# Writing the first batch's front in a fixed order on four engines, with constant tables split on the host

## The chip, the cores and the metric

One core of one Trainium2 chip. The metric is the device time of one execution in microseconds; the time before is the median of three runs. The profile is one further execution, whose engines are TensorE (PE), VectorE (DVE), ScalarE (ACT) and GpSimd (POOL); SyncE (SP) issues the DMAs of before.

## The reference

Eight batches, eight heads, 576 positions, head dimension 64, 32 packing queries; all in fp32. A first attention packs the keys and values with the 32 queries, a second attention reads the packed values with 576 queries. The result, [8, 576, 512], goes through a block that mixes by a two-dimensional Fourier transform and then through a feed-forward network (FFN).

```python
p_packed = sm_attn(p, k, v)
x = sm_attn(q, p_packed, p_packed)        # heads joined: [8, 576, 512]
u = x + real(fft(fft(x, axis=1), axis=2))
un = (u - mean(u)) / sqrt(var(u) + 1e-6)
out = u + relu(un @ w_ch1) @ w_ch2        # 512 -> 2048 -> 512
```

## The kernel before

Products that need more than one reduced-precision pass are made from a hi and a lo part of each operand, in three matmuls (`three`): hi x hi, hi x lo, lo x hi. `split` makes the parts: ACT casts the hi part, DVE or POOL subtracts it for the lo part. On DVE this reads `yl<-py,yh`, on POOL `wr_l<-w1f,wr_h`.

`front(b)` computes one batch from its attention to `u`. The heads are handled in two groups, 0 and 1, of four heads each. The pieces have letters, and the string `ORDER` says in which order they are written: K, V, Q load keys, values and queries; s scores and exponentials of the first attention (`s1`, `e1`), t their transposes, p the packed values (`po`, `pp2`, and the block-diagonal `bd`, `bdh`, `bdl`), d the transposed packed values, q scores of the second attention, e subtraction of the maximum and exponentials (`less_one`), m subtraction of the mean (`less_mean`), a normalisation `s*z` and transpose (`weights`), f sums and differences `eo` and `f` of mirrored positions (`folded`), r small remaining sums (`folded_rest`), h hi and lo parts `fh`, `fl`, `xl`, `ol`, g the cosine and sine spectrum of the values over the columns (`turned`, then `gh`, `gl`), B and T the constant tables `basis` and `tbh`, `tbl`, `tbr`. After the pieces, products `py` of `fh` with `gh` of both groups give `yh`, `yl` and `yr`; products `pz` of those with the tables give the spectrum `spec`, products `px` the values themselves; and `pe`, `qe` are joined to `u` in the buffer `ubuf`. A batch gives four blocks of 128 tokens (two pairs) and half a block of rest (the R rows). `statistics` gives mean and variance of each block: ACT squares (`junk`) and a power on POOL.

The FFN runs over nine tiles of four blocks. For a tile the normalised blocks `un` are transposed on PE (`untp`) and split into `uh` and `ul`. `up(j)` makes 12 matmuls into `ph` and their relu `hh`, `hl`; `down(j-1)` makes 12 matmuls into four accumulators `acc`; j runs from 0 to 15. Behind each, `step(i)` writes the next part of the front of the following batch, so batch 1's front lies in tile 0. Weights arrive as 64-bit numbers, two 32-bit words each (512 KB for 128x512), in `wst` or a spare place (`w1f`, `w2f`, `ubuf`), and are made into fp32 by one ACT and two DVE instructions (`load_weights`, L171); each place is loaded again when DVE has read it. `wsplits` splits each weight chunk into `wr_h` (ACT) and `wr_l` (POOL).

From tile 1 on, the order of each engine's instructions is the order in which the program is written (`manual_schedule`). Batch 0's front and tile 0 with batch 1's front are given to a scheduler, which orders them by its own estimates. The DMAs of SP go out in the order of one queue.

The tables `EN`, `EF`, `ES`, `EO` choose DVE (0) or POOL (1) by batch (first, second, others) and group.

Of the kernel before, what the change touches and what calls it, by code (L numbers as in the profile page):

```python
# [9 lines left out]
F32 = mybir.dt.float32  # L10
# [6 lines left out]
P = 128  # L17
# [21 lines left out]
ORDER = ("K0 I0 K1 B0 V0 V1 Q0 Q1 W0 W1 W2 W3 s0 t0 p0 d0 s1 t1 p1 q0 e0 d1 g0 q1 e1 m0 m1 a0 f0 r0 h0 a1 "  # L39
         "f1 r1 h1 g1 T0",  # L40
# [37 lines left out]
def tile_kernel(ctx, tc, kpT, qT, v, w1, w2, tabC, tabS, tabR, tabB, tabT, sel, ident_d, out):  # L78
# [44 lines left out]

    def load_base():
        nc.sync.dma_start(sels, sel)
        st = load(tabB, [P, 2, N2], "st_base", "wst")
        h = work.tile([P, 2, N2], F32R, tag="tmp", name="base_h", bufs=3)
        nc.scalar.copy(h, st)
        nc.vector.scalar_tensor_tensor(basis, h.bitcast(F32), selC, st, ALU.mult, ALU.add)
        nc.sync.dma_start(turn, tabT)  # L130

    def load_tables():
        for t, d in enumerate((tabC, tabS)):
            st = load(d, [P, 1, KT], "st_tab", (t, 2))
            split(tbh[t], tbl[t], st[:, 0, :])
        st = work.tile([P, 2, 320], F32, tag="wst", name="st_tabr", bufs=2)
        nc.sync.dma_start(st[:101], tabR)
        for t in range(2):

            h = work.tile([P, DM], F32R, tag="tmp", name="tabr_h", bufs=3)  # L140
            nc.scalar.copy(h[:101, :320], st[:101, t, :])
            nc.vector.scalar_tensor_tensor(
                tbr[t][:101], h[:101, :320].bitcast(F32), selA[:101], st[:101, t, :], ALU.mult, ALU.add)
# [25 lines left out]
    def load_weights(j):  # L169

        for n, dst in enumerate((w1f, w2f)):  # L171
            if (j, n) not in fetched:
                fetch(j, n)
            st = fetched.pop((j, n))
            low, high = st[:, :, 0], st[:, :, 1]
            c = dst[:, j, :].bitcast(I32)


            nc.scalar.activation(c.bitcast(F32), high.bitcast(F32), AF.Prelu, scale=REBIAS, alpha=-2.0 ** 32)  # L179
            nc.vector.tensor_scalar(c, c, 3, None, ALU.logical_shift_left)  # L180
            nc.vector.scalar_tensor_tensor(c, low, 29, c, ALU.logical_shift_right, ALU.bitwise_or)  # L181
# [59 lines left out]
    def front(b):  # L241
# [75 lines left out]
        def packed(g):  # L317
# [15 lines left out]
            bd = work.tile([P, 4, D], F32, tag="tmp", name="bd", bufs=3)  # L333
            nc.gpsimd.tensor_tensor(bd, pp2[:, 0:1, :].to_broadcast([P, 4, D]),
                                    bmask.unsqueeze(2).to_broadcast([P, 4, D]), ALU.mult)

            def diagonals():
                bdh[g] = work.tile([P, 4 * D], F32R, tag="bdh", name="bdh")
                bdl[g] = work.tile([P, 4 * D], F32R, tag="bdl", name="bdl")
                split(bdh[g], bdl[g], bd.rearrange("p a d -> p (a d)"), nc.gpsimd)  # L340

            after(1, diagonals)

        def packed_parts(g):
# [10 lines left out]
            nc.vector.tensor_tensor(lo, tp[:, :P], hi.bitcast(F32), ALU.subtract)  # L355
# [44 lines left out]
        def values_spectrum(g):  # L400
# [21 lines left out]

        def weights(g):

            engs[g].tensor_tensor(s2s[g], s2s[g], broadcast(zs[g]), ALU.mult)
# [48 lines left out]
        def folded_parts(g):  # L474
# [17 lines left out]
                 "W": lambda i: fetch(i // 2, i % 2), "D": load_weights}  # L492
# [7 lines left out]
        yh, yl, yr = [], [], []  # L500
        for t, base in enumerate((0, FO)):
# [24 lines left out]
        def spectrum(t, par):  # L526

            pz = bank("pz")
            k0, off = (0, 0) if par is not None else (P, rows.start)
            pars = (0, 1) if par is None else (par,)  # L530
            for i, q in enumerate(pars):
                w = slice(KW * q + k0 - off, KW * q + k0 - off + P)
                three(pz[:, :N2], tbh[t][:, w], tbl[t][:, w], yh[t][:, q, :], yl[t][:, q, :], i == 0, False)
            k0 = KW * par if par is not None else k0
            nc.tensor.matmul(pz[:, :N2], tbr[t][:NRC[t], k0 - off:k0 - off + P], yr[t][:NRC[t]], start=False, stop=True)
            sb = work.tile([P, N2], F32, tag=f"spec{t}", name=f"spec{t}", bufs=1)
            nc.scalar.copy(sb, pz[:, :N2])
            return sb

        def value(ah, al, w):  # L540
            px = bank("px")
            for g in range(2):
                three(px[:, g * 256:(g + 1) * 256], ah[g][:, w], al[g][:, w], bdh[g], bdl[g], True, True)
            return px

        def window(sb, rows):
            w = sb[rows, 0:256]
            return bass.AP(tensor=w.tensor, offset=w.offset, ap=[list(w.ap[0]), [1, 2], [1, 256]])

        allp = slice(0, P)  # L550

        def halves(x):
            return x.rearrange("p (a c) -> p a c", a=2)

        for c in range(2):
            A, Bs = spectrum(0, c), spectrum(1, c)
            yield
            px = value(xh, xl, slice(1 - c, 256, 2))
            pe = work.tile([P, DM], F32, tag="tmp", name="pe", bufs=3)
            nc.vector.tensor_tensor(halves(pe), halves(px), window(A, allp), ALU.add)  # L560
            px = value(oh, ol, slice(1 - c, 256, 2))
# [8 lines left out]
            statistics((b, "O", c))  # L570
            yield (None, "rest")[c]
# [138 lines left out]

    gen0 = front(0)
# [140 lines left out]
```

## Time and profile before

| | us |
|---|---|
| runs | 1027.53, 1029.04, 1028.04 |
| median | 1028.04 |
| span of the profiled execution | 1025.3 |
| PE busy in it | 978.5 (95%) |
| DVE busy | 608.8 (59%) |
| ACT busy | 425.0 (41%) |
| POOL busy | 463.1 (45%) |
| first matmul of the first up-projection `ph` | 62.70 |
| first output of tile 0 issued | 187.99 |

The profile gives, for the profiled execution, a span from the first to the last instruction; the time of a run is measured around that execution, and the median lies 2.7 us above this span. In rows of the timeline the first number is the start from the span's beginning, the second the length, then engine, line, operation, tile written and tiles read, and shapes. In the chain of waits each row is a piece of the work that ended last, with what it waited for ahead of it.

### The profile page before, as it was taken

The page shows a single profiled execution, that of the slowest core. Times are in us where ns is not written, and L with a number is a line of the kernel's source. Part 1 is how long each engine was busy: PE and PEld are TensorE (multiplying, and loading weights), DVE is VectorE, ACT ScalarE, POOL GpSimd, SP SyncE. Part 2 cuts the span into 40 slices and gives each one's busy share as a digit, 9 for nine tenths or more (in the row PEclk, how much of TensorE's full clock was granted, in tenths as well). Part 3 has the DMA queues.
Part 4 walks back from the last instruction along what each step waited for, and adds up shares of the span by engine and source line. Part 5 has one row for each costly group of instructions (what it writes and reads, how often), then busy time and mean ns, then how long its engine had stood idle before and what let it go on. Part 6 is the DMA issues. An engine that isn't in the chain of part 4 may idle for free.

```text
span 1025.3 us, 14876 instructions
## 1 busy us (share of the span) xinstructions
PE 978.5 (95%) x5692; PEld 795.6 (78%) x5692; DVE 608.8 (59%) x1264; ACT 425.0 (41%) x883; POOL 463.1 (45%) x419
## 2 busy tenths in 40 slices
PE   6489889999999999999999999999999999999998
PEld 2367668878877888788887887788778888887886
DVE  3897994559465856677556846594658562114112
ACT  2556454444443434444444435444435343333322
POOL 1535635364335534454345533643355344444443
PEclk9699899999999999999999999999999999999999
DMA  8328440220023000310041002200210000001001
GB/s 329 109 64 280 157 123 1 93 96 1 1 78 111 1 1 34 108 48 1 1 140 49 1 1 93 96 0 1 82 58 0 1 26 17 0 1 43 1 1 42
DMA packets 17742, 58.64 MB, mean 57 GB/s; under 512 B 2081, under 2 KB 2465, under 8 KB 17670
## 3 DMA queue, kind: packets, MB, share of 16 engines
q1 hardware_dynamic: 17670, 57.68, 16.4%
q8 instruction: 45, 0.74, 0.3%
q14 instruction: 27, 0.22, 0.1%
HBM read 48.24 MB, written 9.44 MB: 56 GB/s over the span
## 4 chain that ended last, share of the span: by engine, by line
PE 76%; DVE 11%; ACT 5%; DMA 3%; issue 2%; POOL 2%; ACTq 0%; SPq 0%; DVEq 0%; POOLq 0%
PE ph L647 35%; PE acc L664 30%; DVE ubuf L567 2%; DMA wst<-w 2%; DVE turned L419 1%; ACT hh L653 1%; PE po L326 1%; PE s L269 1%; ACT junk L217 1%; DVE turned L415 1%; POOL wr_l L100 1%; PE e1tp L303 1%; DVE hl L654 1%; ACT wr_h L99 1%; DVE w2f L181 1%
## 5 line engine op out<-in xcount | busy, mean ns | idle before, releaser
L100 POOL TENSOR_TENSOR wr_l<-w1f,wr_h 128x512 fp32r<-128x512 f32 x144 | 190.8, 1325 | 398.9 <-ACT wr_h L99 395.1
L654 DVE SCALAR_TENSOR_TENSOR hl<-ph,hh 128x512 fp32r<-128x512 f32 x144 | 98.8, 686 | 305.3 <-ACT hh L653 305.0
L647 PE MATMUL ph<-uh,wr_h 128*128 128x512 f32 (+1 forms) x580 | 231.5, 399 | 11.8 <-DVE hl L654 9.6
L100 POOL TENSOR_TENSOR wr_l<-w2f,wr_h 128x512 fp32r<-128x512 f32 x144 | 192.4, 1336 | 91.9 <-ACT wr_h L99 91.9
L664 PE MATMUL acc<-wr_l,hh 128*128 128x512 f32 x576 | 227.0, 394 | 3.0 <-POOL wr_l L100 3.0
L647 PE MATMUL ph<-uh,wr_l 128*128 128x512 f32 (+1 forms) x580 | 229.3, 395 | 0.4 <-POOL wr_l L100 0.4
L647 PE MATMUL ph<-ul,wr_h 128*128 128x512 f32 (+1 forms) x580 | 229.3, 395 | 0.2 <-DVE ul L100 0.2
L664 PE MATMUL acc<-wr_h,hh 128*128 128x512 f32 x576 | 227.8, 396 | 0.0
L664 PE MATMUL acc<-wr_h,hl 128*128 128x512 f32 x576 | 226.2, 393 | 0.0
L653 ACT ACTIVATE hh<-ph 128x512 fp32r<-128x512 f32 x144 | 85.8, 596 | 285.6 <-PE ph L647 285.4
L647 PEld LDWEIGHTS ph<-uh,wr_h 128*128 128x128 f32 x580 | 109.9, 190 | 44.9 <-DVE hl L654 9.8
L647 PEld LDWEIGHTS ph<-uh,wr_l 128*128 128x128 f32 x580 | 110.0, 190 | 24.7 <-POOL wr_l L100 0.8
L664 PEld LDWEIGHTS acc<-wr_l,hh 128*128 128x128 f32 x576 | 108.2, 188 | 26.8 <-POOL wr_l L100 5.4
L647 PEld LDWEIGHTS ph<-ul,wr_h 128*128 128x128 f32 x580 | 110.0, 190 | 23.9 <-issue 1.7
L664 PEld LDWEIGHTS acc<-wr_h,hh 128*128 128x128 f32 x576 | 108.2, 188 | 23.5 <-ACT w2f L179 0.8
L664 PEld LDWEIGHTS acc<-wr_h,hl 128*128 128x128 f32 x576 | 108.2, 188 | 23.1
L99 ACT CAST wr_h<-w2f 128x512 fp32r<-128x512 f32 x144 | 89.4, 621 | 9.4 <-PE ph L647 7.8
L99 ACT CAST wr_h<-w1f 128x512 fp32r<-128x512 f32 x144 | 88.4, 614 | 8.0 <-PE ph L647 3.1
L217 ACT ACTIVATE junk<-ubuf,stat 128x512 f32<-128x512 f32 x36 | 25.8, 718 | 77.3 <-DVE stat L213 77.3
L608 PE MATMUL untp<-ident,un 128*128 128x128 f32 x144 | 37.2, 273 | 1.9 <-DVE stat L220 1.7
L100 POOL TENSOR_TENSOR gl<-turned,gh 128x516 fp32r<-128x516 f32 x16 | 25.2, 1573 | 22.1 <-ACT gh L99 22.1
L567 DVE SCALAR_TENSOR_TENSOR ubuf<-qe,pe 128x512 f32<-128x512 f32 x32 | 34.6, 1115 | 0.5
(199 smaller groups left out, 1292.8 us busy)
## 6 DMA issues: line engine op xcount, KB each, us to landing
kp<-kpT SPq DMA_DIRECT2D x16, 608.0 KB, 4.9
out<-ubuf SPq DMA_DIRECT2D x36, 256.0 KB, 2.1
vt<-v SPq DMA_DIRECT2D x14, 640.0 KB, 4.7
wst<-w SPq DMA_DIRECT2D x17, 512.0 KB, 4.0
qt<-qT SPq DMA_DIRECT2D x14, 576.0 KB, 4.8
ubuf<-w SPq DMA_DIRECT2D x9, 512.0 KB, 4.6
w1f<-w SPq DMA_DIRECT2D x3, 512.0 KB, 11.1
w2f<-w SPq DMA_DIRECT2D x3, 512.0 KB, 11.2
```

Of the source, the lines that this page charges most:

```text
L99: nc.scalar.copy(hi, src)
L100: (lo_eng or nc.vector).tensor_tensor(lo, src, hi.bitcast(F32), ALU.subtract)
L181: nc.vector.scalar_tensor_tensor(c, low, 29, c, ALU.logical_shift_right, ALU.bitwise_or)
L217: nc.scalar.activation(junk, u, AF.Square, bias=st[:, 1:2], scale=-1.0, accum_out=st[:, 2:3])
L269: nc.tensor.matmul(res[g][c][at, :w.stop - w.start], lhs(g, h), rhs(g, h, w), start=True, stop=True, tile_position=(r, h * NPK))
L303: nc.tensor.transpose(tp[g][:, c * P:(c + 1) * P], e1s[g][:, c * P:(c + 1) * P], ident)
L567: nc.vector.scalar_tensor_tensor(u_of[key], qe, sign, pe, ALU.mult, ALU.add, accum_out=stat_of[key][:, 0:1])
L608: nc.tensor.transpose(tp[:, c * P:(c + 1) * P], un[:, c * P:(c + 1) * P], ident)
L647: nc.tensor.matmul(ph[:, t], l[:, c * P:(c + 1) * P], r[:, c, t], start=(k == 0), stop=(k == 11))
L653: nc.scalar.activation(hh[:, :T], ph[:, :T], AF.Relu)
L654: nc.vector.scalar_tensor_tensor(hl[:, :T], ph[:, :T], 0.0, hh[:, :T].bitcast(F32), ALU.max, ALU.subtract)
L664: nc.tensor.matmul(acc[i], l[:, w], r, start=(j == 0 and k == 0), stop=(j == NJ - 1 and k == 2))
```

## The change

Batch 0's front and the turning of its four blocks are written under `manual_schedule`, in an order given by the first string of `ORDER`. Tile 0 itself stays with the scheduler.

- New pieces: x exponentials of the first attention apart from its maxima, b `bd` and its parts, l the lo part of the packed values, j the join of the turned spectrum with its parts, w and v the two halves of rebuilding a weight (ACT; DVE), c the parts of `basis`, z the next weight split, P the products `py` of one group. All 18 products of group 0 are written ahead of those of group 1, in six banks.
- The table `EW` is new, and `EF` changed: `s*z` and `eo` of batch 0's group 1 go from POOL to DVE.
- `tbh`, `tbl` and `tbr` are no longer split on the core. Their hi and lo parts come from the host, and six DMAs on POOL's queue load them (4 x 224 KB, 2 x 160 KB); the three loads on SP go.
- `un` of the first four blocks is made by ACT (Identity with the negative mean as bias) instead of DVE.
- The squares and deviations of batch 0's blocks are put off to steps 6 and later of tile 0, and the R rows of batch 0 to its steps 0 and 2.
- The order of loads on SP is another for batch 0.

```diff
-EF = (((0, 0, 0, 0), (1, 1, 0, 0)), ((1, 1, 1, 1), (0, 0, 0, 0)), ((0, 0, 0, 0), (0, 0, 0, 0)))
+EW = ((0, 0), (1, 0), (0, 0))
+EF = (((0, 0, 0, 0), (0, 0, 0, 0)), ((1, 1, 1, 1), (0, 0, 0, 0)), ((0, 0, 0, 0), (0, 0, 0, 0)))
...
-ORDER = ("K0 I0 K1 B0 V0 V1 Q0 Q1 W0 W1 W2 W3 s0 t0 p0 d0 s1 t1 p1 q0 e0 d1 g0 q1 e1 m0 m1 a0 f0 r0 h0 a1 "
-         "f1 r1 h1 g1 T0",
+ORDER = ("K0 K1 V0 I0 Q0 V1 W0 Q1 B0 W1 W2 W3 s0 x0 s1 t0 x1 p0 t1 d0 w0 v0 q0 e0 p1 l0 d1 c0 m0 q1 b0 T0 a0 e1 "
+         "g0 f0 r0 w1 l1 m1 w2 w3 g1 z0 a1 j0 h0 P0 f1 r1 b1 j1 h1 P1",
...
     def load_tables():
-        for t, d in enumerate((tabC, tabS)):
-            st = load(d, [P, 1, KT], "st_tab", (t, 2))
-            split(tbh[t], tbl[t], st[:, 0, :])
-        st = work.tile([P, 2, 320], F32, tag="wst", name="st_tabr", bufs=2)
-        nc.sync.dma_start(st[:101], tabR)
         for t in range(2):
-            h = work.tile([P, DM], F32R, tag="tmp", name="tabr_h", bufs=3)
-            nc.scalar.copy(h[:101, :320], st[:101, t, :])
-            nc.vector.scalar_tensor_tensor(
-                tbr[t][:101], h[:101, :320].bitcast(F32), selA[:101], st[:101, t, :], ALU.mult, ALU.add)
+            nc.gpsimd.dma_start(tbh[t], tabH[t])
+            nc.gpsimd.dma_start(tbl[t], tabL[t])
+            nc.gpsimd.dma_start(tbr[t], tabR[t])
...
-        after(1, squares)
-        after(2, deviation)
+        if steps[0] is None:
+            n = 6 + 2 * len(due) // 2
+            due.extend([(n, squares), (n + 1, deviation)])
+        else:
+            after(1, squares)
+            after(2, deviation)
...
+        def in_place(kind, g, what):
+            if b == 0:
+                late[kind, g] = what
+            else:
+                what()
...
-            engs[g].tensor_tensor(s2s[g], s2s[g], broadcast(zs[g]), ALU.mult)
+            engw[g].tensor_tensor(s2s[g], s2s[g], broadcast(zs[g]), ALU.mult)
...
+        def first_products(g):
+            outs = [(0, 0), (0, 2), (1, 0), (1, 2), (0, 1), (1, 1)]
+            if g == 0:
+                ypx.update({o: bank("py") for o in outs})
...
+            for t, c in outs:
+                py = ypx[t, c]
+                nr, base = NRC[t] if c == 2 else P, (0, FO)[t]
+                w = slice(base + c * P, base + c * P + nr)
+                three(py[:nr, :N2], fh[g][:, w], fl[g][:, w], gh[g][:, t, :], gl[g][:, t, :], g == 0, g == 1)
...
+        if b == 0:
+            ypx["q", 0] = odd_values(0)
+            spec = {(t, c): spectrum(t, c, "wr" if c else None) for c in range(2) for t in range(2)}
+            ypx["p", 1] = value(xh, xl, slice(0, 256, 2))
+            ypx["q", 1] = odd_values(1)
+            for c in range(2):
+                blocks(c, even(c, spec[0, c], ypx["p", c]), spec[1, c], ypx["q", c])
+                yield ("means", "rest")[c]
...
-    for at in gen0:
-        if at == "rest":
-            break
-    cur = Turned(tiles[0][1])
-    for i in range(4):
-        cur.less(i)
-        for move in cur.moves(i):
-            move()
-        cur.parts(i)
-    for _ in gen0:
-        pass
+    def turn_blocks(*ks):
+        for i in ks:
+            key = cur.keys[i]
+            cur.un[i] = work.tile([P, DM], F32, tag="ln", name="un")
+            nc.scalar.activation(cur.un[i], u_of[key], AF.Identity, bias=stat_of[key][:, 1:2])
+        for i in ks:
+            for move in cur.moves(i):
+                move()
+
+    with tc.manual_schedule(engines=MANUAL):
+        for at in gen0:
+            if at == "means":
+                turn_blocks(0, 1)
+            elif at == "rest":
+                break
+        cur.parts(0)
+        cur.parts(1)
+        bits(1, 0)
+        turn_blocks(2, 3)
+        cur.parts(2)
+        cur.parts(3)
+        next(splits)
+        bits(0, 1)
+        bits(1, 1)
...
-    rest = iter(())
+    rest = gen0
...
-            if t > 0 and i in (0, 2):
+            if i in (0, 2):
                 next(rest, None)
```

Three places of the order follow. The first is POOL in batch 0, between the lo part of the first block-diagonal (`bdl`) and the subtraction of the maximum from the second attention's scores of group 1 (L381, which is L410 now). Before:

```order
L100 TENSOR_TENSOR bdl<-bd,bdh 128x256
L334 TENSOR_TENSOR bd<-pp_238,bmask 128x256
L100 TENSOR_TENSOR bdl<-bd,bdh 128x256
L100 TENSOR_TENSOR gl<-turned,gh 128x516
L381 TENSOR_TENSOR s_298<-s_298,m_301 128x576
L397 TENSOR_TENSOR s_298<-s_298,d_314 128x576
```

Now:

```order
L101 TENSOR_TENSOR bdl<-bd,bdh 128x256
L140 DMA tbh_87<-tabH 128x448
L141 DMA tbl_89<-tabL 128x448
L142 DMA tbr_93<-tabR 128x320
L140 DMA tbh_88<-tabH 128x448
L141 DMA tbl_90<-tabL 128x448
L142 DMA tbr_94<-tabR 128x320
L410 TENSOR_TENSOR s_281<-s_281,m_299 128x576
L489 TENSOR_TENSOR f<-eo 128x3x15 x4
```

Group 1's block-diagonal and group 0's `gl` have left this place, and the six table loads stand in it; group 0's small sums stand between the two subtractions of group 1.

The second place is DVE from group 1's lo part `fl` to the first pair of `u` (`s_`, `spec_` and the like carry numbers of the program's buffers). Before:

```order
L485 TENSOR_TENSOR fl<-f,fh 128x776
L100 TENSOR_TENSOR tbl_89<-w1f,tbh_87 128x448
L100 TENSOR_TENSOR tbl_90<-w2f,tbh_88 128x448
L142 SCALAR_TENSOR_TENSOR tbr_93<-tabr_h,sels,st_tabr 101x320
L142 SCALAR_TENSOR_TENSOR tbr_94<-tabr_h,sels,st_tabr 101x320
L100 TENSOR_TENSOR yl<-py,yh 128x258 x2
L518 SCALAR_TENSOR_TENSOR yr<-yr_h,sels,pyr 101x258
L100 TENSOR_TENSOR yl<-py,yh 128x258 x2
L518 SCALAR_TENSOR_TENSOR yr<-yr_h,sels,pyr 99x258
L560 TENSOR_TENSOR pe<-px,spec_487 128x512
L181 SCALAR_TENSOR_TENSOR w1f<-w1f 128x512
L563 TENSOR_TENSOR qe<-px,spec_494 128x256
```

Now:

```order
L519 TENSOR_TENSOR fl<-f,fh 128x776
L101 TENSOR_TENSOR yl<-py,yh 128x258
L585 SCALAR_TENSOR_TENSOR yr<-yr_h,sels,py 101x258
L101 TENSOR_TENSOR yl<-py,yh 128x258
L585 SCALAR_TENSOR_TENSOR yr<-yr_h,sels,py 99x258
L101 TENSOR_TENSOR yl<-py,yh 128x258 x2
L625 TENSOR_TENSOR pe<-px,spec_505 128x512
L630 TENSOR_TENSOR qe<-px,spec_512 128x256
```

The table parts and the weight's bits are gone from this stretch.

The third place is PE around the first up-projection, where `s_706` (now `s_682`) are batch 1's first scores. Before:

```order
L269 MATMUL s1t<-kp 32x64 x4
L269 MATMUL s_706<-kp 32x512 x4
L608 MATMUL untp<-ident,un 128x128 x8
L269 MATMUL s1t<-kp 32x64 x4
L608 MATMUL untp<-ident,un 128x128 x4
L647 MATMUL ph<-uh,wr_h 128x256
L647 MATMUL ph<-ul,wr_h 128x256
L647 MATMUL ph<-uh,wr_l 128x256
```

Now, with the 21 rows of that up-projection from L731 on left out between the two pieces:

```order
L290 MATMUL s1t<-kp 32x64
L731 MATMUL ph<-uh,wr_h 128x256
L290 MATMUL s1t<-kp 32x64 x3
L692 MATMUL untp<-ident,un 128x128 x8
L731 MATMUL ph<-ul,wr_h 128x256
```

```order
L731 MATMUL ph<-uh,wr_l 128x256
L748 MATMUL acc_613<-wr_h,hh 128x512
L748 MATMUL acc_613<-wr_l,hh 128x512
L290 MATMUL s_682<-kp 32x512 x4
L290 MATMUL s1t<-kp 32x64 x4
```

Batch 1's first scores moved from ahead of the up-projection to behind the first two matmuls of the first accumulator, and the R rows' products `px`, which stood ahead of these rows, follow behind the second up-projection.

More of the change, by code (lines that the diff above doesn't have):

```diff
@@ L167, in fetch, with chunk, top, bits @@
         fetched[j, n] = st
-    def load_weights(j):
[L171 to L181, printed above, removed]
+    def chunk(j, n):
+        return (w1f, w2f)[n][:, j, :].bitcast(I32)
+    def top(j, n):
+        if (j, n) not in fetched:
+            fetch(j, n)
+        high, c = fetched[j, n][:, :, 1], chunk(j, n)
+        return nc.scalar.activation(c.bitcast(F32), high.bitcast(F32), AF.Prelu, scale=REBIAS, alpha=-2.0 ** 32)
+    def bits(j, n):
+        low, c = fetched.pop((j, n))[:, :, 0], chunk(j, n)
+        nc.vector.tensor_scalar(c, c, 3, None, ALU.logical_shift_left)
+        nc.vector.scalar_tensor_tensor(c, low, 29, c, ALU.logical_shift_right, ALU.bitwise_or)
+    def load_weights(j):
+        for n in range(2):
+            tc.keep_in_program_order(top(j, n))
+            bits(j, n)
     u_of, stat_of, place_of, free = {}, {}, {}, list(range(NU))
@@ L332, in packed, with spread, diagonals @@
             pp2s[g] = pp2
[L333 to L342, printed above, removed]
+            def spread():
+                bd = work.tile([P, 4, D], F32, tag="tmp", name="bd", bufs=3)
+                nc.gpsimd.tensor_tensor(bd, pp2[:, 0:1, :].to_broadcast([P, 4, D]),
+                                        bmask.unsqueeze(2).to_broadcast([P, 4, D]), ALU.mult)
+                def diagonals():
+                    bdh[g] = work.tile([P, 4 * D], F32R, tag="bdh", name="bdh")
+                    bdl[g] = work.tile([P, 4 * D], F32R, tag="bdl", name="bdl")
+                    split(bdh[g], bdl[g], bd.rearrange("p a d -> p (a d)"), nc.gpsimd)
+                after(1, diagonals)
+            in_place("b", g, spread)
         def packed_parts(g):
@@ new lines, in spectrum @@
+        def spectrum(t, par, tag=None):
+            pz = bank("pz")
+            k0, off = (0, 0) if par is not None else (P, rows.start)
+            pars = (0, 1) if par is None else (par,)
+            for i, q in enumerate(pars):
+                w = slice(KW * q + k0 - off, KW * q + k0 - off + P)
+                three(pz[:, :N2], tbh[t][:, w], tbl[t][:, w], yh[t][:, q, :], yl[t][:, q, :], i == 0, False)
+            k0 = KW * par if par is not None else k0
+            nc.tensor.matmul(pz[:, :N2], tbr[t][:NRC[t], k0 - off:k0 - off + P], yr[t][:NRC[t]], start=False, stop=True)
+            sb = work.tile([P, N2], F32, tag=tag or f"spec{t}", name=f"spec{t}", bufs=6 if tag else 1)
+            copied = nc.scalar.copy(sb, pz[:, :N2])
+            if b == 0 and par is None:
+                tc.keep_in_program_order(copied)
+            return sb
@@ L497, in front @@
                 parts[x[0]](int(x[1:] or 0))
-        yh, yl, yr = [], [], []
-        for t, base in enumerate((0, FO)):
+        for t, base in enumerate((0, FO) if b else ()):
             nr = NRC[t]
@@ L523, in front, with even, blocks @@
             yield
[L526 to L558, printed above, removed]
+        def even(c, A, px):
             pe = work.tile([P, DM], F32, tag="tmp", name="pe", bufs=3)
             nc.vector.tensor_tensor(halves(pe), halves(px), window(A, allp), ALU.add)
-            px = value(oh, ol, slice(1 - c, 256, 2))
+            return pe
+        def blocks(c, pe, Bs, px):
             qe = work.tile([P, DM], F32, tag="tmp", name="qe", bufs=3)
```

104 lines of the change are left out of this document (78 added, 26 removed).

## The prediction

> **What bounds the kernel now.** I read first the busy time by stages (columns: stretch and its length; busy microseconds and instructions of PE, weight loads, DVE, ACT, POOL; granted clock of PE; DMA share; GB/s).
>
> ```profile
> 0.00:63.00 63.00, 36.67 (x301) 24.75 (x301) 43.73 (x107) 28.84 (x67) 20.96 (x49) 0.84 0.52 183
> 63.00:104.00 41.00, 38.92 (x265) 28.73 (x265) 33.14 (x68) 22.29 (x45) 21.21 (x18) 0.96 0.65 220
> 104.00:144.00 40.00, 30.73 (x135) 23.45 (x134) 39.34 (x80) 18.06 (x33) 21.47 (x19) 0.87 0.35 113
> ...
> 188.00:300.00 112.00, 111.17 (x675) 91.48 (x674) 74.20 (x156) 47.12 (x100) 50.10 (x43) 1.00 0.13 47
> ```
>
> ```profile
> 187.99 2.90 SPq L701 DMA_DIRECT2D out<-ubuf  x4
> ```
>
> Until 63 us PE works 36.67 of 63 us; this is batch 0's front. Tile 0 of the FFN follows and ends where SP issues its outputs, at 187.99. From there PE is busy 111.17 of 112 us, and all later tiles have the code of before, so a change can only move that one point, 187.99; the end follows it one to one. Within tile 0, DVE sets the pace from 104 to 144 (39.34 of 40).
>
> Next I read the chain of waits that leads to it (start, length, engine, tile, line).
>
> ```profile
> 28.07 1.17 POOL s L381
> ...
> 36.10 1.19 POOL s L425
> ...
> 38.76 0.69 POOL eo L437
> ...
> 40.10 1.66 POOL f L455 x4
> ...
> 43.62 0.85 ACT fh L479
> ...
> 45.35 1.81 issue
> 47.17 0.68 ACT w1f L179
> 47.85 0.52 ACT yh L99 x2
> ...
> 62.62 0.61 DVE ul L100
> 63.28 3.02 PE ph L647 x23
> 66.32 0.60 ACT hh L653
> ```
>
> Group 1 of batch 0 goes through POOL almost alone from 36 to 43.6, then ACT and an unexplained 1.81, then DVE until ul, and the first up-projection ends in hh at 66.32. The third view is the timeline, DVE's first (in brackets the idle time ahead and what ended it).
>
> ```profile
> 31.36 0.75 DVE L425 TENSOR_TENSOR s<-s,z 128x576 f32<-128x576 f32 x1
> ...
> 34.32 0.42 DVE L437 TENSOR_TENSOR eo<-a 128x287 f32<-128x287 f32 x1
> ...
> 45.38 1.71 DVE L100 TENSOR_TENSOR tbl<-w1f,tbh 128x448 fp32r<-128x448 f32 x1
> 47.01 0.61 DVE L100 TENSOR_TENSOR tbl<-w2f,tbh 128x448 fp32r<-128x448 f32 x1
> 47.54 1.00 DVE L142 SCALAR_TENSOR_TENSOR tbr<-tabr_h,sels,st_tabr 101x320 fp32r<-101x320 f32 x2
> ...
> 51.08 0.69 DVE L560 TENSOR_TENSOR pe<-px,spec 128x512 f32<-128x512 f32 x1 [0.27 <-ACT spec L537]
> 51.68 0.68 DVE L181 SCALAR_TENSOR_TENSOR w1f<-w1f 128x512 int32<-128x512 int32 x1
> 52.45 0.42 DVE L563 TENSOR_TENSOR qe<-px,spec 128x256 f32<-128x256 f32 x1
> ...
> 53.45 0.69 DVE L567 SCALAR_TENSOR_TENSOR ubuf<-qe,pe 128x512 f32<-128x512 f32 x1
> ...
> 54.07 1.79 DVE L567 SCALAR_TENSOR_TENSOR ubuf<-qe,pe 128x512 f32<-128x512 f32 x1
> ...
> 61.10 0.68 DVE L581 TENSOR_TENSOR xa<-px,spec 64x512 f32<-64x512 f32 x1
> ...
> 61.76 0.47 DVE L601 TENSOR_SCALAR un<-ubuf,stat 128x512 f32<-128x512 f32 x1
> ...
> 62.55 1.87 DVE L100 TENSOR_TENSOR ul<-untp,uh 128x512 fp32r<-128x512 f32 x3
> ```
>
> ```profile
> 39.60 0.58 PE L237 MATMUL py<-gh,fh 128*128 128x258 f32 x1 [15.12 <-ACT fh L479]
> 59.70 1.04 PE L269 MATMUL s<-kp 64*32 64x512 f32 x8
> ```
>
> From 51.08 on DVE's rows follow each other without idle time of note up to ul: 51.08 to 64.42 is a stretch that DVE sets.
>
> **The change, part by part.** I use group 1's chain, since group 0's is earlier all along.
>
> 1. The six table transfers on POOL. They stand on POOL between group 0's bdl and group 1's subtraction of the maximum (28.07 before).
>
> ```profile
> 21.70 0.74 POOL L100 TENSOR_TENSOR bdl<-bd,bdh 128x256 fp32r<-128x256 f32 x1 [0.52 <-ACT bdh L99]
> 26.83 1.28 POOL L100 TENSOR_TENSOR gl<-turned,gh 128x516 fp32r<-128x516 f32 x1 [4.39 <-ACT gh L99]
> 32.34 1.20 POOL L397 TENSOR_TENSOR s<-s,d 128x576 f32<-128x576 f32 x1 [3.11 <-DVE d L394]
> ...
> 32.44 1.13 DVE L395 TENSOR_SCALAR z<-z 128x18 f32<-128x18 f32 x1
> ```
>
> ```profile
> 60.80 12.00 SPq L233 DMA_DIRECT2D vt<-v  x2
> 74.81 0.33 SPq L166 DMA_DIRECT2D ubuf<-w  x1
> ```
>
> ```profile
> 78.42 4.81 DMA wst<-w
> ```
>
> ```profile
> 24.00:32.00 8.00, 0.48 (x3) 0.28 (x3) 7.82 (x17) 5.60 (x10) 2.40 (x2) 0.80 1.01 334
> ```
>
> Before, POOL ended both groups' bd and bdl at 22.44 and idled 4.39 us; with group 1's pair gone it is free at about 22.4 - 2 x 0.74 = 20.9. Group 1's maxima are ready near 26 (before: 27.8, with two turned products and a join ahead of them on DVE that now stand behind). So the transfers have 5 us, or 0.85 us each, for nothing. The trace has no DMA issued by POOL. Nearest rows: SP's issue of one DMA, 0.33 us (74.81), and POOL's own arithmetic, 1.2 to 1.3. I take 1.0, inside but nearer the upper end because POOL is the engine in question: subtraction at 20.9 + 6.0 = 26.9 instead of 28.07, a gain of 1.2. Each 0.1 us more costs 0.6. At 0.33 it would start at 26 (0.9 more gained), at 1.3 at 28.7 (1.8 less). The tables are 1.2 MB where the three loads of before were 0.7; the DMA engines are full at that time (1.01 from 24 to 32), so these and the weights beside them land up to 0.5 MB / 334 GB/s = 1.5 us later, hidden as long as the first pz comes near 50 and batch 0 loads nothing after 32 that is wanted before 47.
>
> What could raise the price is shown by the rows at 32.34 and 32.44: a DVE instruction of 18 elements took 1.13 us because it started beside a POOL instruction that ran until 33.54. [...]
>
> 2. Group 1's weights and sums go to DVE. s*z (1.19 on POOL at 36.10, behind 2.6 us of small sums) becomes 0.75 on DVE by the DVE row of the same shape, and eo 0.42 + 0.45 instead of 1.34. Followed through: subtraction 26.9 to 28.1; two exponentials 1.4 and the sum 0.9, 30.4; POOL's sums of group 0 (3.3) stand before s-d, which so starts at 31.4 and ends at 32.6 (before 33.54); s*z and transpose on DVE to 34.1 (before 38.26). But group 0's join, xl, ol and fl (0.84 + 0.42 + 0.43 + 1.34) stand before group 1's eo on DVE: eo ends near 38.0 instead of 40.1. POOL's sums 3.5, so fh ends at 42.4 instead of 44.46. Gain so far 2.1.
>
> 3. Tables removed from ACT and DVE. tbl 1.71 + 0.61 and tbr 1.00 are 3.3 us of DVE directly ahead of the first yl; with the 1.81 of issue and w1f on ACT, they made it 3.4 us from fh's end (44.47) to the first yh (47.85). Now fl (1.0) and gl (1.5) must be done and three matmuls at half clock run: 2.6. First yh at 45.0, gain 2.8.
>
> 4. Order of the products. The 18 products of group 0 ran alone ahead of group 1 already (PE row at 39.60), so writing them so gives nothing. But all 18 of group 1 (0.215 apart in the trace) and one px now stand ahead of the first pz, while before the first pz ran beside them: 45.0 + 3.9 + 1.3 + 0.9 + the copy puts pe at about 51.1, and the gain of 2.8 is used up. Bounds: 0 to 2.8 gained; I take 0, because PE counts 34 matmuls there.
>
> 5. DVE's stretch from pe to ul. Removed from it: two bit steps of the weights (0.68 each) with a shift (0.42), which go to holes and between the ul; four un (1.9), which go to ACT; four deviations (0.56); R's xa and first half (1.1); and the wait of 1.79 - 0.69 = 1.1 behind POOL's weight split. Together 6.8. What remains: two pairs of pe 0.69, qe 0.84, ubuf 2 x 0.69, stat 0.14 = 3.05 each, so the last ubuf is at 51.1 + 6.1 = 57.2; then un on ACT twice 0.6 (ACT's instructions of this size take 0.59 to 0.73), four transposes 0.66, uh 0.6, ul 0.6: 60.2 instead of 64.42. Gain 4.2 (bounds 1.9, if only un counts, and 6.8). PE has to warm up again in this stretch, so hh comes at 62.5, 3.8 earlier than 66.32.
>
> 6. What is moved past the first up-projection. On DVE R's 1.5 and the deviations' 0.6 are now in tile 0, on ACT four squares of 0.72, on PE R's px (0.6), and batch 1's scores of group 0 (1.04 at 59.70 before) now stand behind the first accumulation, which waits for hh.
>
> SP issues batch 1's values only when those scores are done (60.80 before), and the weights stand behind it on SP; a late vt lets a late weight follow, and the chain has waits for weights such as 78.42. I put vt at 64 to 68.
>
> How much of 3.8 arrives at 188? If DVE set the pace of all of tile 0, its 2.1 us more would be taken off: 1.7. If the 7.9 us in which DVE idles between 63 and 104 absorb them: 3.8. I take the middle, 2.7. Three places of the SP queue (three table loads less, 0.33 each near 11 us) are worth nothing, because SP there waits for keys.
>
> **Sum.** 187.99 - 2.7 = 185.3, the profiled span 1025.3 - 2.7 = 1022.6. The median of the runs is 1028.04, 2.7 above that span, so the forecast is 1025.3. What a measurement here can tell from no change is 0.2%, 2.06 us.
>
> **Rivals.**
> A, the forecast: 1.7 to 3.8 us faster, 1024.2 to 1026.3. Chance 0.42, of which 0.08 lies within 2.06 us.
> B, no gain arrives. For it: 39.34 of 40 in DVE's stretch; vt later on SP. Against it: DVE's 7.9 us idle. If vt and the weights start 3 to 4 us later and DVE waits for them as at 78.42, the 2.7 are eaten: 1028. Chance 0.20.
> C, slower: the six transfers on POOL. It decides from 1.45 us each (2.7 / 6 + 1.0). At 2.0 each (a price of 1.0 and a wait of up to 0.75 for the DVE instruction running, with 0.25 of spread) the subtraction stands at 32.9: 6 x 1.0 - 2.7 = 3.3 slower, 1031.3. For it: the wait at 32.44; no row has the price. Against it: that wait was for one instruction, and POOL's own rows there (1.17, 1.20) show no wait for DVE. Chance 0.23, with 0.04 of it above 1032.5. [...]
> D, more than forecast. PE falls to a low clock in tile 0 while it waits for DVE:
>
> ```profile
> 112.00:120.00 8.00, 3.85 (x9) 3.07 (x10) 8.00 (x11) 1.47 (x3) 4.02 (x3) 0.64 0.60 198
> ```
>
> In 112 to 120 the clock was 0.64, so (1 - 0.64) x 8 = 2.9 us of full clock were missing. If batch 1's chain lies otherwise and this stretch does not occur: 2.7 + 2.9 = 5.6 faster, 1022.4. Chance 0.15.
>
> **How the numbers follow.** Faster: 0.42 - 0.08 + 0.15 = 0.49; same: 0.08 + 0.20 = 0.28; slower: 0.23. The range of 8 in 10 reaches down past D (1022.4) by the 1.9 that step 5 leaves open, 1020.5, and up past C by one more 0.2 us per transfer, 1032.5. A's own range is 1024.2 to 1026.3.
>
> **What would show it.** After: POOL's six transfers between bdl and the subtraction, the latter near 26.9; fh's end near 42.4; pe near 51.1; the last ul near 60.2; hh near 62.5; outputs of tile 0 near 185.3; the same 837 us behind them. Wrong if the subtraction comes after 30, if hh is earlier by 3 us or more and the outputs are not, or if later tiles move among themselves.

## The result, and the profile after

The changed kernel took 1021.83 us (median of 4 runs, 1020.61 to 1022.02) against 1027.91 for the kernel before on the same chip: 6.1 us less, ratio 0.994 with a 95% interval of 0.9926 to 0.9954. The forecast was 1025.3, 2.7 less. The profiled execution spans 1020.1 us instead of 1025.3. In these runs the time of a run is its span and about 1.8 us.

The stages of the changed kernel, in the same columns as before, and its first output of tile 0:

```profile
0.00:63.00 63.00, 37.39 (x302) 26.41 (x302) 43.42 (x103) 25.58 (x54) 19.75 (x49) 0.73 0.50 188
63.00:104.00 41.00, 39.73 (x270) 29.36 (x271) 28.46 (x59) 25.62 (x57) 21.14 (x21) 0.96 0.57 180
104.00:144.00 40.00, 34.54 (x155) 26.18 (x153) 38.65 (x82) 18.72 (x35) 22.66 (x20) 0.91 0.46 147
...
188.00:300.00 112.00, 111.19 (x695) 90.87 (x673) 73.68 (x158) 48.37 (x106) 50.26 (x44) 1.00 0.14 46
```

```profile
182.31 2.90 SPq L785 DMA_DIRECT2D out<-ubuf  x4
```

From that output to the end pass 837.8 us (837.3 before), so the gain of the profiled execution lies ahead of it: 187.99 - 182.31 = 5.7. The first hh splits it. It stands at 63.08 (66.32 before): the front gave 3.24. From hh to the output tile 0 takes 119.2 us instead of 121.7: tile 0 gave 2.4, where the forecast had it lose 1.1.

The front, in the rows that the prediction named (POOL's timeline, then DVE's and ACT's):

```profile
20.47 0.99 POOL L101 TENSOR_TENSOR bdl<-bd,bdh 128x256 fp32r<-128x256 f32 x1 [8.12 <-ACT bdh L100]
21.40 0.76 POOL L140 DMA_DIRECT2D tbh<-tabH  x1
22.16 0.55 POOL L141 DMA_DIRECT2D tbl<-tabL  x1
...
24.24 0.58 POOL L142 DMA_DIRECT2D tbr<-tabR  x1
25.86 1.15 POOL L410 TENSOR_TENSOR s<-s,m 128x576 f32<-128x576 f32 x1 [1.04 <-DVE m L409]
...
31.32 1.26 POOL L101 TENSOR_TENSOR wr_l<-w1f,wr_h 128x512 fp32r<-128x512 f32 x1
...
40.88 0.23 POOL L502 TENSOR_SCALAR f<-a 128x31 f32<-128x31 f32 x1
41.19 0.61 POOL L361 TENSOR_TENSOR bd<-pp,bmask 128x256 f32<-128x256 f32 x1
```

```profile
23.54 0.72 DVE L459 TENSOR_TENSOR s<-s,z 128x576 f32<-128x576 f32 x1
...
31.49 1.71 DVE L459 TENSOR_TENSOR s<-s,z 128x576 f32<-128x576 f32 x1
...
37.78 0.44 DVE L472 TENSOR_TENSOR eo<-a 128x287 f32<-128x287 f32 x1
...
51.29 0.69 DVE L625 TENSOR_TENSOR pe<-px,spec 128x512 f32<-128x512 f32 x1 [0.85 <-ACT spec L544]
...
59.17 1.28 DVE L101 TENSOR_TENSOR ul<-untp,uh 128x512 fp32r<-128x512 f32 x2
```

```profile
41.84 0.40 ACT L100 CAST bdh<-bd 128x256 fp32r<-128x256 f32 x1 [3.17 <-POOL bd L361]
42.15 0.62 ACT L100 CAST gh<-turned 128x516 fp32r<-128x516 f32 x1
42.67 0.83 ACT L513 CAST fh<-f 128x776 fp32r<-128x776 f32 x1
...
45.64 0.37 ACT L100 CAST yh<-py 128x258 fp32r<-128x258 f32 x1 [2.13 <-PE py L250]
...
63.08 0.59 ACT L737 ACTIVATE hh<-ph 128x512 fp32r<-128x512 f32 x1
```

The six transfers took POOL 3.4 us together, and POOL then idled 1.04 us until DVE had the maxima: they cost nothing here. s*z of group 1, now on DVE, ran 1.71 instead of 0.75: it started beside POOL's weight split of 31.32 and ended 0.62 after that split's end at 32.58.

In tile 0, PE's waits for DVE's hl from 62 us to the end of tile 0, before and after (us in total, times, longest), and ACT's waits for weights that were still on their way:

```profile
PE ph L647 <- DVE hl L654: 9.6, 3, 4.4
```

```profile
PE ph L731 <- DVE hl L738: 4.2, 2, 2.4
```

```profile
ACT w1f L179 <- DMA wst<-w: 7.3, 6, 3.6
...
ACT w2f L179 <- DMA wst<-w: 6.4, 6, 2.0
```

```profile
ACT w2f L177 <- DMA wst<-w: 3.0, 2, 1.9
```

PE lost 5.4 us less to hl, and the weights were hardly waited for any more. These rows say where time was won, not why; the experiments ask that.

### The profile page after: what moved, and what is told of

It reads as the page before. It is cut to its first block, busy times and chain, and to the rows that moved or that the text cites. A ratio compares the mean times of both kernels' runs of the same rounds, so it can differ in the third digit from the quotient of the medians.

```text
span 1020.1 us, 14869 instructions
## 1 busy us (share of the span) xinstructions
PE 978.4 (96%) x5692; PEld 795.6 (78%) x5692; DVE 604.5 (59%) x1259; ACT 425.7 (42%) x883; POOL 457.8 (45%) x422
## 4 chain that ended last, share of the span: by engine, by line
PE 79%; DVE 12%; ACT 5%; issue 2%; POOL 1%; DMA 0%; ACTq 0%; DVEq 0%; POOLq 0%
PE ph L731 35%; PE acc L748 32%; DVE ubuf L634 2%; DVE turned L451 1%; DVE turned L445 1%; PE po L351 1%; ACT hh L737 1%; ACT junk L224 1%; POOL wr_l L101 1%; PE s L290 1%; DVE hl L738 1%; PE e1tp L328 1%; PE py L248 1%; PE py L250 1%; PE py L249 1%
## 5 line engine op out<-in xcount | busy, mean ns | idle before, releaser
L101 POOL TENSOR_TENSOR wr_l<-w1f,wr_h 128x512 fp32r<-128x512 f32 x144 | 187.4, 1301 | 407.7 <-ACT wr_h L100 406.8
L731 PE MATMUL ph<-uh,wr_h 128*128 128x512 f32 (+1 forms) x580 | 231.6, 399 | 6.5 <-DVE hl L738 4.2
L731 PE MATMUL ph<-uh,wr_l 128*128 128x512 f32 (+1 forms) x580 | 229.5, 396 | 0.0
L731 PE MATMUL ph<-ul,wr_h 128*128 128x512 f32 (+1 forms) x580 | 229.3, 395 | 0.1
L731 PEld LDWEIGHTS ph<-uh,wr_h 128*128 128x128 f32 x580 | 110.0, 190 | 40.8 <-issue 8.4
L731 PEld LDWEIGHTS ph<-uh,wr_l 128*128 128x128 f32 x580 | 109.9, 190 | 24.0
L731 PEld LDWEIGHTS ph<-ul,wr_h 128*128 128x128 f32 x580 | 110.1, 190 | 23.2 <-issue 0.8
L101 DVE TENSOR_TENSOR ul<-untp,uh 128x512 fp32r<-128x512 f32 x36 | 23.8, 685 | 15.9 <-ACT uh L100 15.9
```

Of the source, the lines that this page charges most:

```text
L101: (lo_eng or nc.vector).tensor_tensor(lo, src, hi.bitcast(F32), ALU.subtract)
L731: nc.tensor.matmul(ph[:, t], l[:, c * P:(c + 1) * P], r[:, c, t], start=(k == 0), stop=(k == 11))
```

## Experiments

All are compared with the kernel before on their chip (medians of 1027.4 to 1028.0), by the ratio of their runs (95% interval). hh is the start of the first hh, length the time from there to the first output of tile 0, both of the profiled execution. What follows tile 0 took 836.8 to 838.3 us in every kernel.

| kernel | time | ratio | hh | length |
|---|---|---|---|---|
| before | 1027.91 | | 66.32 | 121.7 |
| changed | 1021.83 | 0.994 [0.9926, 0.9954] | 63.08 | 119.2 |
| twelve | 1029.14 | 1.0016 [1.0006, 1.0026] | 70.37 | 119.7 |
| un_dve | 1026.70 | 0.9988 [0.9978, 0.9997] | 68.71 | 119.2 |
| pool_g1 | 1024.25 | 0.9963 [0.9949, 0.9976] | 65.75 | 119.3 |
| front_sched | 1017.60 | 0.9897 [0.9873, 0.9921] | 60.32 | 114.4 |
| squares_in | 1026.18 | 0.9989 [0.9979, 0.9998] | 69.12 | 118.1 |
| rest_in | 1020.50 | 0.9924 [0.9909, 0.9939] | 65.82 | 115.9 |
| tables_only | 1028.97 | 1.0006 [0.9993, 1.002] | 70.14 | 118.8 |
| defer_only | 1030.66 | 1.0024 [1.001, 1.0037] | 66.32 | 126.3 |
| tile0_written | 1034.34 | 1.0065 [1.0049, 1.008] | 63.52 | 133.2 |
| fs_rest | 1017.72 | 0.9906 [0.9888, 0.9923] | 61.04 | 115.4 |
| fs_un_dve | 1019.82 | 0.992 [0.9893, 0.9947] | 64.96 | 117.3 |
| small_first | 1024.22 (1 run) | | 66.28 | 117.8 |

The profiled execution of front_sched (1014.25) was its fastest and 3.4 below its median, so its hh and length flatter it by 3.4 us together. That of fs_rest was 1.7 below its median, that of fs_un_dve 2.0 above. And in the written kernels rows that no edit touches start at different times: group 0's last bdl at 19.90 (small_first) to 21.59 (pool_g1), 20.47 in the changed kernel. Where this matters, hh is counted below from a row ahead of the edit.

**twelve: what a transfer on POOL costs.**

```diff
+    extra = cpool.tile([P, 6, 8], F32, name="extra")
...
             nc.gpsimd.dma_start(tbr[t], tabR[t])
+        for i in range(6):
+            nc.gpsimd.dma_start(extra[:, i, :], tabT[:, i // 3, i % 2, 0:8])
```

> The changed kernel with six more small transfers on POOL behind the six tables (128 x 8 elements each, into a tile that nothing reads). Six cost 3.4 us in the trace of the changed kernel (21.40 to 24.82) and POOL then idled 1.04 us, so the subtraction of group 1 moves from 25.86 to about 28.1. If POOL's transfers are priced as in the prediction (each microsecond beyond the slack lies on the path), hh comes about 2.0 later, at 65.1, and the time is about 1023.8. Rival: group 1's chain has further slack on DVE (turned products and sums of group 0 lie between), then hh moves by under 0.7 and the time stays within 1 us of 1021.8.

The subtraction moved by 8.1 to 33.98, hh by 7.3, the time by 7.3. So the place is on the path: what exceeds the slack arrives almost whole, as rival C had it. Its price was something else, as POOL's timeline shows:

```profile
24.20 0.56 POOL L143 DMA_DIRECT2D tbr<-tabR  x1
24.72 0.59 POOL L145 DMA_DIRECT2D extra<-tabT  x1
28.75 0.55 POOL L145 DMA_DIRECT2D extra<-tabT  x1 [3.44 <-issue]
30.47 0.53 POOL L145 DMA_DIRECT2D extra<-tabT  x1 [1.17 <-issue]
```

Seven transfers went out 0.55 apart; the eighth stood 3.44 us.

**small_first: why the eighth waits.** The same, with the six small transfers ahead of the tables.

> The kernel twelve with its six small transfers ahead of the six tables instead of behind. In twelve the eighth transfer began only at 28.75, 3.4 us after the seventh, when the first table (224 KB, issued at 21.40) may have landed. If POOL may have only so many transfers under way (seven), the small ones land early (3.1 us in twelve) and free the places: the subtraction comes near 21.4 + 12 x 0.56 + 1 = 29 instead of 33.98. If every transfer beyond the seventh waits the same, the subtraction is near 34 again.

```profile
20.83 3.41 POOL L141 DMA_DIRECT2D extra<-tabT  x6
24.24 0.54 POOL L143 DMA_DIRECT2D tbh<-tabH  x1
26.31 0.54 POOL L144 DMA_DIRECT2D tbl<-tabL  x1 [1.53 <-issue]
...
29.30 1.17 POOL L413 TENSOR_TENSOR s<-s,m 128x576 f32<-128x576 f32 x1
```

Again the eighth is the first to wait, but only 1.53 us: the small ones land sooner (5.1 us from issue by the median, the tables of twelve 8.2 to 9.0), and the subtraction is at 29.30, as expected of seven places. In both runs seven go out without such a wait, whatever their size, and the landings in the traces say what ends the wait of the eighth. In twelve the first five transfers landed at 28.44, 30.16, 31.35, 32.56 and 33.13, and the eighth to the twelfth began 0.31 us after them, at 28.75, 30.47, 31.66, 32.87 and 33.44; in small_first the eighth began 0.32 after the first had landed (25.99). So in these two runs, with seven under way, the next one went out when the oldest had landed. The change with its six stayed one below that.

**un_dve: un of the first four blocks on DVE.**

```diff
-            nc.scalar.activation(cur.un[i], u_of[key], AF.Identity, bias=stat_of[key][:, 1:2])
+            nc.vector.tensor_scalar(cur.un[i], u_of[key], stat_of[key][:, 1:2], None, ALU.add)
```

> The changed kernel with un of the first four blocks on DVE again. Four times 0.47 = 1.9 us come back into the stretch of DVE from pe to ul, less what ACT's un (0.67 each) took in latency. If DVE sets that stretch: hh about 1.3 later (64.4), time about 1023.1 with a tile 0 as long as now (119.2 from hh to the first output). Rival: the chain through un, transposes and uh sets it; then hh is earlier by up to 0.4 and the time 1021.5.

hh moved by 5.6, four times what I expected. DVE's rows and PE's transposes show where:

```profile
52.76 0.69 DVE L625 TENSOR_TENSOR pe<-px,spec 128x512 f32<-128x512 f32 x1 [0.84 <-ACT spec L544]
...
59.23 1.28 DVE L101 TENSOR_TENSOR ul<-untp,uh 128x512 fp32r<-128x512 f32 x2
60.43 0.42 DVE L181 TENSOR_SCALAR w1f<-w1f 128x512 int32<-128x512 int32 x1
60.88 0.69 DVE L182 SCALAR_TENSOR_TENSOR w1f<-w1f 128x512 int32<-128x512 int32 x1
61.49 0.88 DVE L803 TENSOR_SCALAR un<-ubuf,stat 128x512 f32<-128x512 f32 x2
64.42 1.51 DVE L101 TENSOR_TENSOR ul<-untp,uh 128x512 fp32r<-128x512 f32 x2 [2.06 <-ACT uh L100]
```

```profile
62.71 1.88 PE L692 MATMUL untp<-ident,un 128*128 128x128 f32 x8
```

In this execution pe came at 52.76, 1.5 later than in the changed kernel and ahead of any un; so un on DVE is worth 4.2. The second pair's u was ready at 59.0, but its un stands in the written order behind the first pair's ul and a weight, 2.5 us; and the second pair's ul comes only at 64.42. On ACT, un passed that queue. The work was 1.8 us. PE's clock adds to it: its transposes of the second pair took 1.88 us, at a granted clock of 0.56 from 60.7 to 64.6, instead of 1.27 at 1.00 (57.74 in the changed kernel). How the 4.2 divide among work, queue and clock was not separated.

**pool_g1: s\*z and eo of group 1 on POOL again.**

```diff
-EW = ((0, 0), (1, 0), (0, 0))
-EF = (((0, 0, 0, 0), (0, 0, 0, 0)), ...
+EW = ((0, 1), (1, 0), (0, 0))
+EF = (((0, 0, 0, 0), (1, 1, 0, 0)), ...
```

> The changed kernel with s*z and eo of group 1 on POOL again (EW and EF of batch 0 as before). By the rows: s*z 1.19 instead of 0.75, eo 1.34 instead of 0.87, behind group 0's lo part on POOL; hh 1 to 2 later and time 1023 to 1024. The rest of the kernel's order is the same but for eight rows, so this shows also whether tile 0's length (119.2 us from the first hh to the first output, 121.7 before the change) depends on when it starts: if it was shortened by its order it stays at 119.2 +- 0.7; if by its start, it goes back towards 121.7 in proportion (about 120.5).

hh 2.7 later, time 2.4 higher. In this profile 1.1 of the 2.7 lie ahead of the edit (group 1's subtraction at 26.98 instead of 25.86), so the edit is worth 1.6 in hh here and 2.4 by the medians.

It also bears on the length. In twelve, un_dve and pool_g1 tile 0 starts 2.7 to 7.3 later than in the changed kernel and takes 119.2 to 119.7 us; in twelve and pool_g1 PE's, ACT's and SP's orders are the changed kernel's row for row. So a later start neither lengthens nor shortens tile 0. But the order does not fix the length: small_first has the same rows in the same order and takes 117.8. Its second hh comes 7.4 us after the first, in the changed kernel 8.9. The same six microseconds after the first hh, in the changed kernel and in small_first:

```profile
65.00:71.00 6.00, 6.00 (x35) 3.18 (x34) 3.10 (x9) 3.04 (x8) 1.49 (x1) 0.72 0.37 112
```

```profile
68.20:74.20 6.00, 6.00 (x44) 3.35 (x44) 4.25 (x12) 3.59 (x10) 1.47 (x1) 1.00 0.47 121
```

PE is busy throughout in both, at a granted clock of 0.72 and of 1.00. The 1.5 us are still there at the output (1.4). Twelve, pool_g1 and the kernel before also show 0.72 there; why small_first does not stays open.

**tile0_written: the same work, another order of tile 0.**

```diff
-        with tc.manual_schedule(engines=MANUAL) if t > 0 else nullcontext():
+        with tc.manual_schedule(engines=MANUAL):
```

> The changed kernel with tile 0 also under the written order. hh stays near 63 (the front is the same). If tile 0's length is a matter of its order: another length than 119.2, from the lengths seen so far (114.4 to 126.3) it can go either way; PE's written order puts both of batch 1's scores ahead of the second up-projection, so the first accumulation comes 2 us later, but DVE's weights come in step: 117 to 123, time 1019 to 1026. If the length is set by the sum of DVE's work (94 us in before and after alike), it stays within 0.7 of 119.2 and the time within 1 us of 1021.8.

```profile
135.00:150.00 15.00, 4.87 (x19) 3.16 (x17) 14.36 (x44) 5.99 (x11) 6.41 (x9) 0.73 0.37 119
```

```profile
PE py L248 <- ACT fh L513: 7.7, 1, 7.7
PE s L290 <- ACT e L317: 3.6, 1, 3.6
```

The first row is the stretch from 135 to 150, the other two are PE's longest waits in the whole of tile 0. hh hardly moved (63.52), and tile 0 takes 133.2: 14 us more from the order alone. From 135 to 150 PE works 4.87 of 15 us. The wait of 7.7 us ends at 149.16: PE stands at one product of batch 1 whose `fh` is not ready, and the next up- and down-projection, whose last parts (`wr_l`, `hl`) are there at 144.6 and 145.8, stand behind it. The clock fell with the waits, to 0.89 over tile 0 instead of 0.96. So the length is a matter of the order, not of the sum of work.

**front_sched: the written front given back to the scheduler, all else kept.**

```diff
-    with tc.manual_schedule(engines=MANUAL):
+    with nullcontext():
         for at in gen0:
```

> The changed kernel with batch 0's front given to the scheduler again, all else (tables from the host, engines, un on ACT, squares and rest rows put off) kept. If the written order brings the front's 3.2 us: hh near 66, time 1024.5 to 1028. If the removed and moved work brings it: hh near 63, time within 1 us of 1021.8.

This is the fastest kernel: 4.2 us below the changed one, with intervals that do not meet. Neither expectation held; the written order, which names the change, loses. POOL's rows show one part:

```profile
1.25 0.76 POOL L140 DMA_DIRECT2D tbh<-tabH  x1 [0.43 <-issue]
...
4.58 0.54 POOL L142 DMA_DIRECT2D tbr<-tabR  x1
```

```profile
22.48 1.62 POOL L410 TENSOR_TENSOR s<-s,m 128x576 f32<-128x576 f32 x1 [0.83 <-DVE z L424]
```

The scheduler issues the tables at POOL's idle start and brings group 1's subtraction 3.4 us forward. Tile 0 is 4.8 shorter in its profile; the clock stays at 1.00 at its start, which in small_first came with a second hh 1.5 us earlier.

**squares_in: squares and deviations in the front** (no putting off in `statistics`).

> The changed kernel with the squares and deviations of batch 0's four blocks left in the front (ACT four times 0.72, DVE four times 0.14, POOL four small powers). If ACT is now on the path of the turning (un 0.67 and uh 0.6 each): hh 1.5 to 3 later, 64.6 to 66; tile 0, which is ordered anew without them, 118 to 119.5 long; time 1023 to 1025. Rival: they fit into ACT's idle 1.5 us ahead of un, hh within 0.7 and the time within 1 us of 1021.8.

hh 6.0 later for 2.9 us of ACT, with pe where it was (51.38): squares that wait for their mean stand on ACT ahead of un and uh of the pair (second un at 61.87 instead of 56.96), and from 62 to 66 PE then runs at a granted clock of 0.57.

**rest_in: the rest rows ahead of tile 0.**

```diff
         next(splits)
+        for _ in gen0:
+            pass
         bits(0, 1)
```

> The changed kernel with the rest rows of batch 0 worked off ahead of tile 0 (PE 20 matmuls, ACT two copies, DVE 1.5 us). If the putting off is worth what the prediction's step 5 said: hh 1 to 2 later (64 to 65) and tile 0 shorter by up to as much, time 1021.8 to 1023.8. If tile 0's length hangs on the order that the scheduler happens to find: length anywhere from 114 to 122 and the time follows it.

hh is 2.7 later, of which 1.1 lie ahead of the rest rows (pe at 52.41). Tile 0 is 3.4 shorter, and the clock stays at 1.00 at its start here too. The time is 1.3 lower by the medians, with intervals that overlap: putting the rest rows off shows no gain.

**tables_only and defer_only: one part alone, on the kernel before.** The first takes only the tables from the host, the second only puts off the squares and rest rows; both leave the order to the scheduler.

> The kernel before with nothing but the tables: hi and lo from the host by six transfers on POOL, order by the scheduler (it puts the transfers at POOL's very start, where POOL idles until 17). By step 3 of the prediction 3.3 us of DVE ahead of the first yl go: pe 1 to 3 earlier than 51.08, hh 63.3 to 65.3. With a tile 0 as long as before (121.7) the time is 1025 to 1027; if tile 0 is ordered otherwise, its length differs and the time follows it. Against: 1.2 MB at the start delays the keys and queries, and hh comes later than 66.32.

> The kernel before with nothing but the putting off: squares and deviations of batch 0's blocks and its rest rows go to tile 0, order by the scheduler. By step 5: 0.56 + 1.1 us of DVE and 2.9 us of ACT leave the stretch, hh 1.5 to 2.5 earlier (63.8 to 64.8). With tile 0 as long as before the time is 1025.5 to 1026.5; if the putting off is what shortens tile 0 (119.2 in the changed kernel, 114.4 with the scheduler's front), its length is below 119 here too and the time 1019 to 1024.

Neither gains. In tables_only the scheduler fills DVE's free place with other work ahead of the first yl:

```profile
45.61 0.68 DVE L175 SCALAR_TENSOR_TENSOR w1f<-w1f 128x512 int32<-128x512 int32 x1
46.21 1.50 DVE L174 TENSOR_SCALAR w2f<-w2f 128x512 int32<-128x512 int32 x1
47.64 1.51 DVE L174 TENSOR_SCALAR w1f<-w1f 128x512 int32<-128x512 int32 x1
49.07 0.68 DVE L175 SCALAR_TENSOR_TENSOR w2f<-w2f 128x512 int32<-128x512 int32 x1
```

That is 4 us of weights in place of 3.3 us of tables. In defer_only hh did not move, and tile 0 came out 4.7 longer. So the 10 us of front_sched are not the sum of parts that were run alone; the new order of loads on SP was never run by itself.

**fs_rest and fs_un_dve: the two edits again, on front_sched.**

> The kernel front_sched (scheduler's front, 1017.6) with the rest rows ahead of tile 0 as in rest_in. In rest_in this cost 2.7 in hh and gave 3.4 in tile 0. If it adds up the same way: hh near 63, tile 0 near 111, time 1016.9. If the scheduler's tile is merely another draw: length 112 to 122, time 1016 to 1026.

> The kernel front_sched with un of the first four blocks on DVE. In the written order this cost 5.6 us of hh, because un of the second pair stood behind two ul and a weight on DVE. If that was the queue and not the work, the scheduler avoids it and hh moves by 1.9 us at most from 60.3 (to 62.2), time 1017.6 to 1020. If un on ACT is worth 5 us by itself, hh is near 66 and the time near 1023.

fs_rest is the same as front_sched within their intervals; the sum did not add up (length 115.4, not 111), so a length under another order is a new draw. In fs_un_dve un on DVE costs 2.2 us by the medians (the intervals overlap) where it cost 4.9 in the written order. Its hh is 4.6 later, more than the 1.9 expected, but 3.9 of that stand at pe already (49.25 instead of 45.34), ahead of any un. From pe to hh pass 15.7 us instead of 15.0, where the written order lost 4.2. This fits that much of the 4.2 was the queue; the spread of these runs (1016.64 to 1021.83) allows no more.

## Why the prediction was partly right

Step 1, the transfers: 0.55 us each instead of 1.0, and the slack of 5 us was there. The subtraction came at 25.86 (forecast 26.9), set by DVE's maxima at 25.7. The rows show no transfer that waited for DVE, though DVE ran `tensor_tensor` instructions beside them (22.17 and 23.54, 0.69 and 0.72 us). Beside POOL's arithmetic two rows of DVE did take longer: before, z took 1.13 us at 32.44, where POOL subtracted, and 0.16 at 29.51, where POOL was idle, and now s*z took 1.71 instead of 0.75 beside POOL's weight split (31.49). Rival C was out by price, but its slope was right: twelve crossed to the slower side.

Step 2: fh ended at 43.50 (42.4). Beside that split s*z took 1.0 more, but eo still ended at 38.22 (38.0) and POOL's sums at 41.11 (41.5). What came late is fh itself: the written order puts bdh and gh of group 1 ahead of it on ACT, bdh waits for POOL's bd, and fh starts only at 42.67, a wait that the forecast did not have. The edit alone was put at 0.9 (2.1 less the 1.2 of step 1); pool_g1 gives 1.6 to 2.4.

Steps 3 and 4: first yh 45.64 (45.0), pe 51.29 (51.1). The half clock of step 3 is the 0.50 granted from 42 to 48 in the kernel before; in the changed kernel it was 1.00 from 43 to 45 and 0.50 from 46 to 48. That the order of PE uses up what the tables free was right to 0.2 us.

Step 5: last ul ends at 60.45 (60.2), hh at 63.08 (62.5). The sum held (its list of removed parts adds up to 6.4 and not 6.8, which touches only the upper bound), but I called these parts DVE's and ACT's time. un_dve and squares_in show that taking un or the squares out is worth 4.2 and 5.9 each in this order, more than the front's whole gain: in a written queue they hold up what stands behind them. The warm-up of PE that step 5 counts was not in this stretch: the granted clock was 1.00 from 51 to 63 in the changed kernel, and before it was 0.50 from 30 to 49 and 1.00 from 50 to 63. hh came 2.6 after the last ul because it stood on ACT behind a `wr_h` that waited 2.40 us for DVE's `w2f` and ran from 62.55; the last row of ph ends at 62.09.

Step 6 is the one that failed. I let the 2.1 us moved into tile 0 take 1.1 of the 3.8 back. hh gained 3.24, and tile 0 then gained 2.4 more. DVE was as busy from 104 to 144 (38.65 of 40), but PE worked 34.54 us there instead of 30.73. I treated tile 0 as a fixed order with more work in it; the scheduler orders it anew whenever anything ahead of it changes. Across the kernels its length went from 114.4 to 133.2. With one order it took 119.2 to 119.7 over starts 7 us apart, and 117.8 in small_first, where the clock did not fall at its start. A forecast from durations had no hold on that term; its error, 3.5 us, was larger than that of all steps before it (0.6 in hh).

D gave 1022.4 and so came nearest to the time, by a smaller loss of clock: the granted clock from 104 to 144 was 0.91 instead of 0.87, (0.91 - 0.87) x 40 = 1.6 us. But clock lost there need not arrive. The changed kernel ran at 0.51 from 123.9 to 127.4 and small_first, with the same order, did not fall there: at the tenth hh its lead, counted from the first, had grown from 1.5 to 2.9 us, at the eleventh it was 1.0 and at the output 1.4. So D's mechanism is not shown to have paid anything. That the time lies inside the range, 1020.5 to 1032.5, is in part luck: the lower end was drawn from D and from what step 5 left open, and by these runs the difference came from neither.

What stays open is which rows of the new order save the 2.4 us. It is not the start (pool_g1) and not the clock at the start of tile 0 (0.72 before and after); that it is the order, and not the work that was moved, is argued from tile0_written and not shown. PE's shorter waits for hl and ACT's for weights fit, but front_sched, with a shorter tile 0, waits longer for hl (6.1) and alike for weights (3.0), and no run moved those rows alone.

## What to carry to other kernels

Split the time at a point that both kernels share (here the first hh and the first output): a part whose order is chosen by a scheduler is a draw that any edit ahead of it repeats, and its spread (114.4 to 126.3 here, and 117.8 to 119.7 with one order) belongs in the range. In a hand-written order, what an edit takes away can be worth the queue behind it and not only its own length, so test every written order against the scheduler's with the same edits: here the edits gained 10 us under the scheduler and 6 under the written order. Count the transfers on a POOL queue, not only their bytes: here the eighth went out only when the first had landed (0.31 us after in twelve, 0.32 in small_first).

## What was not expected of the hardware

A transfer took POOL 0.53 to 0.59 us (the first 0.76 in the changed kernel), whether of 224 KB or 4 KB. The eighth waited 3.44 us behind tables (twelve) and 1.53 behind small transfers (small_first), in both until 0.31 to 0.32 us after the first had landed. And SP needed 0.33 for one (before, 74.81) where POOL needed 0.55. The granted clock of PE, busy throughout, was 0.72 over six microseconds at the start of tile 0 in three kernels and 1.00 in a fourth with PE's rows in the same order, where tile 0 was 1.4 us shorter.
